# First-layer token blocks of 512 and 384 in turn instead of 448, and buffers handed to the second layer by name

## The chip, the cores and the metric

One core of one Trainium2 chip. The metric is device time in microseconds (us) of one execution. TensorE (PE in the profile) does the matrix products, VectorE (DVE) and ScalarE (ACT) the elementwise work, GpSimd (POOL) almost nothing, and SyncE (SP) issues all DMA transfers.

## The reference

Attention over 4 batches, 8 heads, 576 positions and 64 features per head, with two kinds of masks (a local window of 32, and every 32nd position), and then two feed-forward layers over all 4 x 576 = 2304 tokens with 512 features and 2048 hidden units:

```python
attn_out = _attn_ref(**attn_kwargs)                     # masked softmax attention
x = attn_out.transpose(0, 2, 1, 3).reshape(B * S, H * D)   # 2304 x 512
h = x @ w_in                                            # first layer, 512 -> 2048
g = h * np.tanh(softplus(h))
x = (g @ w_out).astype(np.float32)                      # 2048 -> 512
h = x @ w2_in                                           # second layer
g = h - np.tanh(h)
out = (g @ w2_out).astype(np.float32)
```

The weights of both layers come as 64-bit floats and are turned into 32-bit ones on the chip.

## The kernel before

**Arithmetic.** Every 32-bit operand of a large product is split into a high part and a rest in TensorE's reduced 32-bit format, and each product is the sum of three matmuls: high by high, rest by high, high by rest. So a tile names pairs: `xh`/`xl` (input of a layer, high and rest), `gh`/`gl` (hidden activations, high and rest), `w` (both parts in one tile).

**First layer.** The 2304 tokens are cut into blocks: two of 256 tokens, then four of 448 (`blocks[0]`, L262). The hidden dimension is cut into 16 chunks of 128 (`NC`). A *step* is one block and one chunk (`step`, L841). Its first product (`gemm1`, L849, the matmuls of L855) adds up 4 parts of the input features with 3 matmuls each, into a PSUM bank `h`; the block's tokens are the columns that are streamed, the weights are stationary. ScalarE makes the activation `B` (L874), `gh` is a copy of it (L451 on VectorE or L449 on ScalarE), `gl` a subtraction (L455 on VectorE). The second product (`gemm2`, L900, the matmuls of L906) streams `gh` and `gl` against 4 weight tiles, again 3 matmuls each, into four PSUM banks `acc0` to `acc3` that add up over the 16 chunks. So a step has 12 + 12 matmuls of as many columns as its block has tokens. On TensorE the first product of a step alternates with the second product of the step two before (`LAG`). After a block's last chunk the four banks are moved out (`ev`, L922) and stored.

**Attention** is laid between the steps of the first blocks; it ends in the middle of the second block of 448.

**Second layer.** Blocks of 512 tokens, four of them, and one of 256 (`blocks[1]`). A *unit* (`unit`, L1227) is one block and 256 hidden units. Its first product (L1244) is done in seven products of a two-by-two scheme with 6 matmuls of 256 columns each, into banks `hx`; sums of these on VectorE give `H`; then `th` = tanh (L1332, ScalarE), `H - th` (L1337, VectorE), and `gh`, `gl` as above. Its second product (L1381) has `gh`/`gl` as stationary operand and streams 512 columns of weights, 12 matmuls for each half `i` of the unit, into the same four banks `acc0` to `acc3`.

**Places.** Tiles share places by tags. A step `s` writes `B{s%2}`, `gh{s%2}`, `gl{s%2}`. A unit writes, for its half `i`, `H` into `B{i}`, `th` and later `gl` into `gl{i}`, `gh` into `gh{i}`. So the first unit's half 0 takes the places that the step before the last left, and half 1 those of the very last step, whose second product reads `gh1` and `gl1` to its end. The input of a block sits in `xh{J%2}`, `xl{J%2}` (L800, L801), and `tiles` (L1146) puts the second layer's input into these and some other places.

**Order.** The program is written by a planner (`Plan`, L55). Each piece of work is a task with a cost on each engine that could do it, a key (when it is due), the tasks that it comes after and the places that it takes. `run` (L131) repeatedly takes the task that can start first by these costs and writes it to its engine. Each engine then does its instructions strictly in the order written; real dependences (also those on places) are kept by semaphores whatever the planner thought. `pe_cost` (L218) is its cost of a matmul, `due` (L356 to L366) the due times. A unit takes what its predecessor left from the tables `g_free` (the task after which the places `gh` and `gl` are free) and `t_done` (the one after which `B` is free): `old = g_free.get((prev, i))` and `low1, low2`. Only units enter themselves there, so for the very first unit, whose predecessor is a step of the first layer, both are empty, and the planner takes its places to be free.

Of the kernel before, what the change touches and what calls it, by code (L numbers as in the profile page):

```python
# [9 lines left out]
F32R = mybir.dt.float32r  # L10
# [46 lines left out]
class Plan:  # L57
# [15 lines left out]
    def add(self, engs, fn, key, after=(), take=(), give=(), dma=None, start=0.0, rows=128, table=None, bulk=False):  # L73
        t = Task(engs, fn, key, take, give, dma, start)
        t.bulk = bulk
        t.table = table
        t.seq, t.rows = len(self.tasks), rows
        for a in after:
            if a is not None:
                t.wait += 1  # L80
                a.next.append(t)
        self.tasks.append(t)
        return t
# [132 lines left out]


def pe_cost(n):  # L218
    return 0.0004375 * n + 0.007


def act_cost(n, psum=False, extra=0):
# [11 lines left out]
def copies(n, psum=False):  # L234
    return {ACT: act_cost(n, psum), DVE: dve_cost(n, not psum)}


def pairs_of(n):
    return {DVE: dve_cost(n)}
# [3 lines left out]
def attention_two_moe(  # L243
# [14 lines left out]
    KC = DM // 128  # L258
    NC = 16
    WIN = 32  # L260
    scale = 1.0 / float(D) ** 0.5
    blocks = [[256, 256, 448, 448, 448, 448], [512] * 4 + [256]]  # L262
    TB = 448
    LAG = 2

    const = ctx.enter_context(tc.tile_pool(name="const", bufs=1))
# [18 lines left out]
    def sb(shape, dt, slot, name):  # L285
        return one.tile(shape, dt, tag=slot, name=name)
# [66 lines left out]
    NU, HALF = NC // 2, 256  # L353
# [4 lines left out]
    for l, j, c in steps:  # L358
        if l == 0 and j == 0:
            t_ = max(t_, FIRST + PACE * c)  # L360
        due.append(t_)
        if l == 0:
            t_ += 24 * pe_cost(blocks[l][j]) + (ATTEND if 1 < j < 5 else 0.0)
        else:
            t_ += (42 if blocks[1][j] > HALF else 24) * pe_cost(HALF) + 6 * blocks[1][j] // 128 * pe_cost(DM)
# [81 lines left out]
    def copy(e, out, in_):  # L447
        if e == ACT:
            nc.scalar.activation(out=out, in_=in_, func=ACTF.Copy)  # L449
        else:  # L450
            nc.vector.tensor_copy(out=out, in_=in_)  # L451

    def two(e, out, a, b, op):
        eng = nc.gpsimd if e == POOL else nc.vector
        eng.tensor_tensor(out=out, in0=a, in1=b, op=op)  # L455

    def sub(e, out, a, b):
        two(e, out, a, b, ALU.subtract)
# [330 lines left out]
    xh, xl = {}, {}  # L789
# [3 lines left out]
    def x_split(l, j, p, after, src, buf, key):  # L793
        n = blocks[l][j]
        J = len(blocks[0]) * l + j
        old = [] if J < 2 else [last_g1[J - 2]]

        def high(e):
            if J not in xh:
                xh[J] = sb([128, KC, TB], F32R, f"xh{J % 2}", "xh")  # L800
                xl[J] = sb([128, KC, TB], F32R, f"xl{J % 2}", "xl")  # L801
            copy(e, xh[J][:, p, :n], src())

        def low(e):
            sub(e, xl[J][:, p, :n], src(), xh[J][:, p, :n].bitcast(F32))

        a = add(copies(n), high, key, list(after) + old, give=[buf])
        b = add(pairs_of(n), low, key, [a], give=[buf])
        split.setdefault(J, {})[p] = (a, b)
# [29 lines left out]
    g1_end, B_done, g2_end = {}, {}, {}  # L839
# [271 lines left out]
    xq = {}  # L1111
    x_ready = {}

    def unit_of(place, k):

        if len(place) == 1:
            return place[0][1][:, k:k + 1]
        return place[k][1]

    def factors(j, key, ready):  # L1120
        J = len(blocks[0]) + j
        t0 = starts[1][j]
        old = [last_g1[J - 2]] + list(ready)
        raw = {}

        def load_of(x):

            lower, half = x
            a0 = t0 + HALF * half
            cut = []  # L1130
            for i, (a, m) in enumerate(pieces2):
                lo, hi = max(a, a0), min(a + m, a0 + HALF)
                if lo < hi:
                    cut.append((i, lo, hi, a))
            buf = Buf(TMP, 2 if x == X22 else 1)

            def load(e):
                raw[x] = t = sb([128, 2, HALF], F32, buf.slot, "xraw")
                for k in range(2):
                    for i, lo, hi, a in cut:  # L1140
                        nc.sync.dma_start(out=t[:, k, lo - a0:hi - a0], in_=x2d[2 * lower + k, i][:, lo - a:hi - a])

            after = [x2_store[2 * lower + k, 0, i[0] + 1] for k in range(2) for i in cut] + old
            return add({SP: 0.9 * len(cut)}, load, key - 5 + len(raw_loads), after, take=[buf], dma=0.7), buf

        def tiles():  # L1146

            if J in xq:
                return xq[J]
            one_ = lambda t: [(slice(0, 2), t)]  # L1150
            two_ = lambda a, b: [(slice(0, 1), a), (slice(1, 2), b)]
            cols = lambda t: t.rearrange("p (k n) -> p k n", n=HALF)
            a, b = (sb([128, 7, HALF], F32R, f"x{x}{J % 2}", "xq") for x in "hl")
            hi = [one_(t[:, 2 * i:2 * i + 2]) for t in (a, b) for i in range(3)] + [two_(a[:, 6:], b[:, 6:])]
            if J % 2 == 0:
                slots = ("q0", "q1", "k0", "k1", "xr0")
                lo = [one_(sb([128, 2, HALF], F32R, slot, "xq")) for slot in slots]
                t = sb([128, 4, HALF], F32R, "v", "xq")
                lo += [one_(t[:, :2]), one_(t[:, 2:])]
            else:  # L1160
                t = sb([128, 9, HALF], F32R, "pp", "xq")
                lo = [one_(t[:, 2 * i:2 * i + 2]) for i in range(4)]
                lo += [one_(cols(W2[u, 3][:, 1, :])) for u in (2 * NS, 2 * NS + 1)]
                lo += [two_(*(sb([128, 1, HALF], F32R, f"pT{i}", "xq") for i in range(2)))]
            xq[J] = list(zip(hi, lo))
            return xq[J]

        X11, X12, X21, X22 = (0, 0), (0, 1), (1, 0), (1, 1)
        raw_loads = {}
        plain = blocks[1][j] == HALF  # L1170
        for x in (X11, X21) if plain else (X11, X12, X22, X21):
            raw_loads[x] = load_of(x)
        ld = {x: r[0] for x, r in raw_loads.items()}
        bufs = {x: r[1] for x, r in raw_loads.items()}
        pc, cc = pairs_of(2 * HALF), copies(2 * HALF)
        out_ = {}

        def parts_of(i, x, after, key, last):


            def high(e):
                for k, t in tiles()[i][0]:
                    copy(e, t, raw[x][:, k])

            def low(e):
                hi, lo = tiles()[i]
                if len(hi) == len(lo):
                    for (k, h), (_, t) in zip(hi, lo):
                        sub(e, t, raw[x][:, k], h.bitcast(F32))
                else:  # L1190
                    for k in range(2):
                        sub(e, unit_of(lo, k), raw[x][:, k:k + 1], unit_of(hi, k).bitcast(F32))

            h = add(cc, high, key, after)
            out_[i] = add(pc, low, key + .1, [h], give=[bufs[x]] if last else ())
            return out_[i]

        def combine(o, a, b, after, key, give=()):
            return add(pc, lambda e: two(DVE, raw[o], raw[a], raw[b], ALU.subtract), key, after, give=give)

        x_ready[J] = out_
        if plain:
            for i, x in enumerate((X11, X21)):
                parts_of(i, x, [ld[x]] + old, key + .5 * i, True)
            return


        x11 = parts_of(0, X11, [ld[X11]] + old, key, False)
        t1 = combine(X11, X12, X11, [x11, ld[X12]], key + .2)
        t3 = combine(X12, X22, X12, [t1, ld[X22]], key + .3)  # L1210
        x22 = parts_of(2, X22, [ld[X22]] + old, key + .4, False)
        t2 = combine(X22, X22, X11, [t3, x22], key + .5)
        parts_of(4, X22, [t2], key + .6, True)
        parts_of(5, X12, [t3], key + .7, True)
        parts_of(3, X11, [t2], key + .8, True)
        x21 = parts_of(1, X21, [ld[X21]] + old, key + .9, False)
        t4 = combine(X21, X21, X22, [x21, t2], key + 1, [bufs[X22]])
        parts_of(6, X21, [t4], key + 1.1, True)
# [6 lines left out]
    t_done, g_free = {}, {}  # L1225
# [188 lines left out]
    with tc.manual_schedule():  # L1414
# [23 lines left out]
        for J in range(2, last + 1):  # L1438
# [5 lines left out]
            if J == last:  # L1444

                d5, ends = due[NC * J], [x_store[p, B - 1] for p in range(KC)]
                x = y = None
# [7 lines left out]
        for u in range(NU):  # L1455
# [4 lines left out]
            home(u, 2, [g2_end[at]], k_, d + 8)  # L1460
            home(u, 3, [g2_end[at + 1]], k_, d + 12)
        s2 = NC * (last + 1)
        done_i = [x for k in kept_i.values() for x in k]
        done_o = [x for k in kept_o.values() for x in k]
        more = [done_i + done_o + ends, done_i + done_o + [w2_in[u, 3] for u in (2 * NS, 2 * NS + 1)]]
# [9 lines left out]
        x, y = LATE  # L1475
# [58 lines left out]
```

## Time and profile before

| | us |
|---|---|
| median of 3 runs (904.09 to 904.32) | 904.22 |
| the profiled execution's own time | 905.22 |
| its span, first to last instruction | 903.4 |
| TensorE busy in the span | 892.1 (99%) |
| VectorE busy | 585.3 (65%) |
| ScalarE busy | 424.1 (47%) |

The mean granted clock of TensorE is 0.996 of full speed. Matmuls are pipelined: a matmul's listed duration is the time from its start to the modelled end of its own data, longer than the distance to the next one's start. What one costs in a row of matmuls is therefore read from starts, or from the chain of work, which lists how long a run of matmuls kept the engine.

### The profile page before, as it was taken

Reading aid. Unit: us, or ns where it says so; the run is one execution under the profiler, and the core shown is the slowest. Engines: PE = TensorE matmul, PEld = TensorE weight load, DVE = VectorE, ACT = ScalarE, POOL = GpSimd, SP = SyncE. Lnnn points to the kernel's source line nnn. Section 1 sums busy time; section 2 is a strip of 40 time slices with the busy share of each in tenths; the row PEclk is TensorE's granted clock in tenths of the full one; section 3 lists DMA queues with packets and bytes.
Section 4 is the critical chain, followed back from the end, with each engine's and each line's share of the span. In section 5 each row is a group of like instructions: output and inputs, shape, how many; then the busy total and the mean of one; then the engine's idle time right before and its main releaser. Section 6 shows DMA issues by size and latency. Waiting matters only on the chain.

```text
span 903.4 us, 16481 instructions
## 1 busy us (share of the span) xinstructions
PE 892.1 (99%) x6080; PEld 800.5 (89%) x6080; DVE 585.3 (65%) x1562; ACT 424.1 (47%) x928; POOL 2.4 (0%) x13
## 2 busy tenths in 40 slices
PE   8999999999999999999999899999999999999998
PEld 7899999888888899999999889998989999899897
DVE  6999978655455658777777466575458455545543
ACT  6999987645455525444544242242224222322211
POOL 1000000000000000000000000000000000000000
PEclk9999999999999999999999989999999999999999
DMA  9981122512131059888975253352335233644532
GB/s 292 376 344 37 48 92 88 165 53 64 53 114 43 5 208 297 272 256 272 295 225 171 77 164 105 106 178 102 103 113 181 94 111 123 198 153 167 174 127 71
DMA packets 85233, 138.19 MB, mean 153 GB/s; under 512 B 11104, under 2 KB 38752, under 8 KB 85152
## 3 DMA queue, kind: packets, MB, share of 16 engines
q1 hardware_dynamic: 85152, 137.14, 45.7%
q8 instruction: 48, 0.79, 0.3%
q14 instruction: 33, 0.27, 0.1%
HBM read 107.22 MB, written 29.88 MB: 152 GB/s over the span
## 4 chain that ended last, share of the span: by engine, by line
PE 91%; ACT 3%; DMA 3%; DVE 1%; SPq 1%; issue 0%; ACTq 0%
PE acc L1381 22%; PE acc L906 21%; PE h L855 21%; PE hx L1244 18%; PE hx L1261 3%; PE ops L715 2%; PE sps L589 2%; PE ptps L697 1%; DMA kT<-in_k_dram 1%; ACT L193 1%; DMA stwo<-in_moe_w_out_dram 1%; ACT p L645 1%; DMA stwi<-in_moe_w_in_dram 1%; DMA qT<-in_q_dram 0%; DMA vs<-in_v_dram 0%
## 5 line engine op out<-in xcount | busy, mean ns | idle before, releaser
L855 PE MATMUL h<-xh,wi 128*128 128x448 f32 (+1 forms) x768 | 219.3, 346 | 0.9 <-ACT B L874 0.9
L906 PE MATMUL acc<-gh,wo 128*128 128x448 f32 (+1 forms) x768 | 198.4, 344 | 0.0
L1381 PE MATMUL acc<-w,gh 128*128 128x512 f32 x576 | 181.2, 396 | 2.9 <-ACT ev L922 2.9
L1244 PE MATMUL hx<-xq,w 128*128 128x256 f32 x1280 | 174.3, 285 | 0.0
L1244 PEld LDWEIGHTS hx<-xq,w 128*128 128x128 f32 x1280 | 168.1, 191 | 6.7
L855 PEld LDWEIGHTS h<-xh,wi 128*128 128x128 f32 x768 | 139.2, 189 | 12.6 <-ACT B L874 1.5
L906 PEld LDWEIGHTS acc<-gh,wo 128*128 128x128 f32 x768 | 134.1, 189 | 10.4
L855 PE MATMUL h<-xl,wi 128*128 128x448 f32 (+1 forms) x384 | 130.3, 339 | 0.1
L906 PE MATMUL acc<-gl,wo 128*128 128x448 f32 (+1 forms) x384 | 130.1, 339 | 0.0
L1381 PEld LDWEIGHTS acc<-w,gh 128*128 128x128 f32 x576 | 104.2, 190 | 22.1 <-ACT ev L922 3.8
L1381 PE MATMUL acc<-w,gl 128*128 128x512 f32 x288 | 113.1, 393 | 0.0
L1332 ACT ACTIVATE th<-hx 128x256 f32<-128x256 f32 x48 | 18.5, 385 | 163.6 <-PE hx L1244 123.8
L874 ACT ACTIVATE B<-h 128x448 f32<-128x448 f32 (+1 forms) x96 | 46.8, 491 | 95.5 <-PE h L855 90.7
L1337 DVE SCALAR_TENSOR_TENSOR H<-hx,th 128x256 f32<-128x256 f32 x48 | 20.3, 424 | 104.3 <-ACT th L1332 104.2
L455 DVE TENSOR_TENSOR gl<-B,gh 128x448 fp32r<-128x448 f32 (+1 forms) x96 | 53.2, 555 | 50.0 <-ACT gh L449 47.9
L1332 ACT ACTIVATE th<-H 128x256 f32<-128x256 f32 (+1 forms) x64 | 33.4, 524 | 98.1 <-PE acc L1381 50.7
L455 DVE TENSOR_TENSOR H<-H,hx 128x256 f32<-128x256 f32 x160 | 66.9, 418 | 16.5 <-PE hx L1244 9.0
L855 PEld LDWEIGHTS h<-xl,wi 128*128 128x128 f32 x384 | 72.6, 189 | 4.3 <-DVE xl L455 0.3
L906 PEld LDWEIGHTS acc<-gl,wo 128*128 128x128 f32 x384 | 72.4, 189 | 4.5
L193 ACT ACT_TABLE_LOAD x58 | 74.4, 1283 | 1.0
L1381 PEld LDWEIGHTS acc<-w,gl 128*128 128x128 f32 x288 | 54.6, 190 | 12.4 <-DVE gl L455 0.2
L1337 DVE SCALAR_TENSOR_TENSOR H<-H,th 128x256 f32<-128x256 f32 (+1 forms) x64 | 35.6, 558 | 44.0 <-ACT th L1332 44.0
(117 smaller groups left out, 1026.7 us busy)
## 6 DMA issues: line engine op xcount, KB each, us to landing
w<-w2o SPq DMA_DIRECT2D x160, 256.0 KB, 2.8
stwi<-in_moe_w_in_dram SPq DMA_DIRECT2D x16, 512.0 KB, 8.4
stwo<-in_moe_w_out_dram SPq DMA_DIRECT2D x16, 512.0 KB, 9.0
w2v<-in_moe_w_out_dram SPq DMA_DIRECT2D x32, 256.0 KB, 3.7
w2o<-p SPq DMA_DIRECT2D x48, 128.0 KB, 3.2
w<-w2i SPq DMA_DIRECT2D x24, 256.0 KB, 2.8
out_dram<-ev SPq DMA_DIRECT2D x18, 256.0 KB, 3.9
w2v<-in_moe_w_in_dram SPq DMA_DIRECT2D x8, 512.0 KB, 4.4
```

The costliest lines, as they stand in the source:

```text
L193: self.load_table(t.table)
L455: eng.tensor_tensor(out=out, in0=a, in1=b, op=op)
L589: nc.tensor.matmul(s[a][:, at_, :], tq[64 * a:64 * a + 64, q0:q0 + nq], tk[64 * a:64 * a + 64, k0_:k0_ + nk], start=not lean, stop=not lea ...
L715: nc.tensor.matmul(o[64 * hh:64 * hh + 64, u - u0, :], vv, h["pT", a][:, at_, :], start=True, stop=True,)
L855: nc.tensor.matmul(h_ps[s], w[:, wp, kc, :], xx[:, kc, :n], start=(kc == first_kc and i == 0), stop=(kc == last_kc and i == 2),)
L874: nc.scalar.activation(out=b_tile(), in_=h_ps[s], func=ACTF.Mish, scale=2.0 ** -8)
L906: nc.tensor.matmul(acc[f][:, cols], w[:, wp, 128 * f:128 * f + 128], g, start=(opens and i == 0), stop=(closes and i == 2),)
L1244: nc.tensor.matmul(st[t], w[:, wp, 256 * i + 128 * k:256 * i + 128 * k + 128], unit_of(xq[J][x][xp], k)[:, 0], start=(q in (1, 6, 7, 5) an ...
L1261: nc.tensor.matmul(st[t], w[:, wp], unit_of(xq[J][kc // 2][xp], kc % 2)[:, 0], start=(kc == 0 and m == 0), stop=(kc == KC - 1 and m == 2),)
L1332: nc.scalar.activation(out=st["th", i][:, cols], in_=x, func=ACTF.Tanh, scale=2.0 ** -8)
L1337: nc.vector.scalar_tensor_tensor(out=st["H", i][:, cols], in0=x, scalar=2.0 ** -8, in1=st["th", i][:, cols], op0=ALU.mult, op1=ALU.subtract,)
L1381: nc.tensor.matmul(acc[f], g[:, 128 * f:128 * f + 128], where[wp](), start=(opens and m == 0), stop=(closes and m == 2),)
```

## The change

Four edits. The late blocks of the first layer are 512, 384, 512, 384 tokens instead of 448 each, so blocks of even number have 512 and those of odd number 384; the input tiles `xh0`, `xl0` become larger and `xh1`, `xl1` smaller. `tiles` places the second layer's input accordingly (even blocks no longer use the place `xr0`, odd ones do, and no longer use the places of the attention's `pT`). The planner's cost of a matmul is a table for 256, 384 and 512 columns. And the last two steps of the first layer are entered in `g_free` and `t_done`, as if they were the two halves of a unit.

```diff
--- before.py
+++ after.py
@@ -216,7 +216,7 @@
 
 
 def pe_cost(n):
-    return 0.0004375 * n + 0.007
+    return {256: 0.12, 384: 0.174, 512: 0.227}.get(n, 0.0004375 * n + 0.007)
 
 
 def act_cost(n, psum=False, extra=0):
@@ -259,8 +259,8 @@
     NC = 16
     WIN = 32
     scale = 1.0 / float(D) ** 0.5
-    blocks = [[256, 256, 448, 448, 448, 448], [512] * 4 + [256]]
-    TB = 448
+    blocks = [[256, 256, 512, 384, 512, 384], [512] * 4 + [256]]
+    TB = (512, 384)
     LAG = 2
 
     const = ctx.enter_context(tc.tile_pool(name="const", bufs=1))
@@ -797,8 +797,8 @@
 
         def high(e):
             if J not in xh:
-                xh[J] = sb([128, KC, TB], F32R, f"xh{J % 2}", "xh")
-                xl[J] = sb([128, KC, TB], F32R, f"xl{J % 2}", "xl")
+                xh[J] = sb([128, KC, TB[J % 2]], F32R, f"xh{J % 2}", "xh")
+                xl[J] = sb([128, KC, TB[J % 2]], F32R, f"xl{J % 2}", "xl")
             copy(e, xh[J][:, p, :n], src())
 
         def low(e):
@@ -1150,14 +1150,15 @@
             one_ = lambda t: [(slice(0, 2), t)]
             two_ = lambda a, b: [(slice(0, 1), a), (slice(1, 2), b)]
             cols = lambda t: t.rearrange("p (k n) -> p k n", n=HALF)
-            a, b = (sb([128, 7, HALF], F32R, f"x{x}{J % 2}", "xq") for x in "hl")
-            hi = [one_(t[:, 2 * i:2 * i + 2]) for t in (a, b) for i in range(3)] + [two_(a[:, 6:], b[:, 6:])]
+            m = TB[J % 2] // 128
+            a, b = (sb([128, 2 * m, HALF], F32R, f"x{x}{J % 2}", "xq") for x in "hl")
+            hi = [one_(t[:, 2 * i:2 * i + 2]) for t in (a, b) for i in range(m)]
             if J % 2 == 0:
-                slots = ("q0", "q1", "k0", "k1", "xr0")
-                lo = [one_(sb([128, 2, HALF], F32R, slot, "xq")) for slot in slots]
+                lo = [hi.pop()] + [one_(sb([128, 2, HALF], F32R, slot, "xq")) for slot in ("q0", "q1", "k0", "k1")]
                 t = sb([128, 4, HALF], F32R, "v", "xq")
                 lo += [one_(t[:, :2]), one_(t[:, 2:])]
             else:
+                hi += [one_(sb([128, 2, HALF], F32R, "xr0", "xq"))]
                 t = sb([128, 9, HALF], F32R, "pp", "xq")
                 lo = [one_(t[:, 2 * i:2 * i + 2]) for i in range(4)]
                 lo += [one_(cols(W2[u, 3][:, 1, :])) for u in (2 * NS, 2 * NS + 1)]
@@ -1460,6 +1461,8 @@
             home(u, 2, [g2_end[at]], k_, d + 8)
             home(u, 3, [g2_end[at + 1]], k_, d + 12)
         s2 = NC * (last + 1)
+        for i in range(2):
+            g_free[s2 - 1, i], t_done[s2 - 1, i] = g2_end[s2 - 2 + i], B_done[s2 - 2 + i]
         done_i = [x for k in kept_i.values() for x in k]
         done_o = [x for k in kept_o.values() for x in k]
         more = [done_i + done_o + ends, done_i + done_o + [w2_in[u, 3] for u in (2 * NS, 2 * NS + 1)]]
```

The number of matmuls stays: 16 chunks x 24 for each of the four late blocks, 1536 before and after, half of them now of 512 columns and half of 384.

Where the new order differs most is the hand-over between the layers. On ScalarE before, from the first tanh of the second layer (L1332) to the last move out of the first layer's banks (L922); `hx_6317` and `H_6337` belong to half 0 of the first unit, `H_6356` to its half 1, `hx_6399` and later names to the second unit:

```order
L1332 ACTIVATE th_6389<-hx_6317 128x256
L1332 ACTIVATE th_6407<-H_6356 128x512
L1332 ACTIVATE th_6389<-H_6337 128x256
L449 ACTIVATE gh_6436<-H_6337 128x512
L922 ACTIVATE ev_6448<-acc_5643 128x448
L449 ACTIVATE H_6454<-hx_6399 128x256
L922 ACTIVATE ev_6457<-acc_5655 128x448
L922 ACTIVATE ev_6463<-acc_5661 128x448
L922 ACTIVATE ev_6471<-acc_5672 128x448
```

The same stretch of the changed kernel, where `th_6389` is half 0 and `th_6463` half 1 of the first unit (line numbers are one higher behind L1153):

```order
L1333 ACTIVATE th_6389<-hx_6289 128x256
L1333 ACTIVATE th_6389<-H_6317 128x256
L449 ACTIVATE w2_6345<-w2_6345 128x256
L449 ACTIVATE H_6439<-hx_6398 128x256
L922 ACTIVATE ev_6444<-acc_5662 128x384
L922 ACTIVATE ev_6451<-acc_5669 128x384
L1333 ACTIVATE th_6463<-H_6360 128x512
L922 ACTIVATE ev_6471<-acc_5675 128x384
L922 ACTIVATE ev_6474<-acc_5681 128x384
```

Half 1's tanh stood second, ahead of half 0's second piece and of all four moves out (`ev`); now half 0's two pieces come first, and two of the four moves out stand ahead of half 1's tanh.

On VectorE before, from the first `H - th` to the last `gl` of the first unit (`H_6337` is half 0, `H_6356` half 1):

```order
L1337 SCALAR_TENSOR_TENSOR H_6337<-hx_6317,th_6389 128x256
L1337 SCALAR_TENSOR_TENSOR H_6356<-H_6356,th_6407 128x512
L1337 SCALAR_TENSOR_TENSOR H_6337<-H_6337,th_6389 128x256
L451 CAST gh_6434<-H_6356 128x512
L455 TENSOR_TENSOR gl_6438<-H_6356,gh_6434 128x512
L455 TENSOR_TENSOR gl_6443<-H_6337,gh_6436 128x512
```

And with the change (`H_6317` is half 0, `H_6360` half 1; `w2` tiles are second-layer weights brought in for later units):

```order
L1338 SCALAR_TENSOR_TENSOR H_6317<-hx_6289,th_6389 128x256
L1338 SCALAR_TENSOR_TENSOR H_6317<-H_6317,th_6389 128x256
L455 TENSOR_TENSOR w2_6345<-w2_6345 128x256
L451 CAST gh_6425<-H_6317 128x512
L455 TENSOR_TENSOR gl_6434<-H_6317,gh_6425 128x512
L455 TENSOR_TENSOR H_6439<-H_6439,hx_6407 128x256
L451 CAST w2_6380<-w2_6380 128x512
L455 TENSOR_TENSOR w2_6380<-w2_6380 128x512
L1338 SCALAR_TENSOR_TENSOR H_6360<-H_6360,th_6463 128x512
L451 CAST gh_6481<-H_6360 128x512
L455 TENSOR_TENSOR gl_6488<-H_6360,gh_6481 128x512
```

Half 0 went through behind half 1; now half 0 is finished, with its `gh` and `gl`, before half 1's subtraction.

## Rows read from the trace of the kernel before

**Rows 1.** The page's busy times: TensorE.

```profile
PE 892.1 (99%) x6080; PEld 800.5 (89%) x6080; DVE 585.3 (65%) x1562; ACT 424.1 (47%) x928; POOL 2.4 (0%) x13
```

**Rows 2.** The page's chain that ended last, shares of the span by engine.

```profile
PE 91%; ACT 3%; DMA 3%; DVE 1%; SPq 1%; issue 0%; ACTq 0%
```

**Rows 3.** The chain in order of time (start us, us, what), four runs of matmuls.

```profile
83.97 1.44 PE acc L906 x12
...
342.91 2.48 PE acc L906 x12
...
565.71 2.75 PE acc L1381 x12
...
863.03 2.87 PE hx L1261 x24
```

**Rows 4.** TensorE's timeline (start us, us, instructions), 559.80 to 562.55 us.

```profile
559.80 0.63 PE L1381 MATMUL acc<-w,gh 128*128 128x512 f32 x2
...
561.19 0.62 PE L1381 MATMUL acc<-w,gh 128*128 128x512 f32 x2
...
562.55 3.16 PE L1244 MATMUL hx<-xq,w 128*128 128x256 f32 x24
```

**Rows 5.** TensorE's timeline between attention work, nine matmuls from 184.30 to 186.12 us.

```profile
184.30 0.56 PE L906 MATMUL acc<-gh,wo 128*128 128x448 f32 x2
...
186.12 0.41 PE L697 MATMUL ptps<-ident,p 96*128 96x96 f32 x3
```

**Rows 6.** Stretches: us, PE, PEld, DVE, ACT, POOL busy (instructions), PE clock, DMA.

```profile
166.00:326.00 160.00, 160.00 (x1065) 139.03 (x1064) 86.50 (x349) 81.62 (x126) 0.00 (x0) 1.00 0.23 75
326.00:503.95 177.95, 177.95 (x862) 161.60 (x861) 134.64 (x311) 82.70 (x174) 0.00 (x0) 1.00 0.77 249
422.00:503.95 81.95, 81.95 (x398) 74.42 (x397) 59.84 (x134) 38.64 (x81) 0.00 (x0) 1.00 0.73 234
```

**Rows 7.** The chain in order of time at the hand-over between the layers.

```profile
514.63 2.45 PE acc L906 x12
...
517.11 0.64 ACT th L1332
...
517.77 1.04 DVE H L1337 x2
...
518.83 0.63 ACT gh L449
519.46 0.44 ACT ev L922
...
519.94 5.70 PE acc L1381 x12
525.65 2.51 PE hx L1244 x18
```

**Rows 8.** ScalarE's timeline at the hand-over, idle time before a row in brackets.

```profile
510.30 0.38 ACT L1332 ACTIVATE th<-hx 128x256 f32<-128x256 f32 x1 [2.27 <-PE hx L1244]
517.11 0.94 ACT L1332 ACTIVATE th<-H 128x512 f32<-128x512 f32 x2 [6.42 <-PE acc L906]
518.83 0.63 ACT L449 ACTIVATE gh<-H 128x512 fp32r<-128x512 f32 x1 [0.79 <-DVE H L1337]
519.37 0.53 ACT L922 ACTIVATE ev<-acc 128x448 f32<-128x448 f32 x1
520.57 0.38 ACT L449 ACTIVATE H<-hx 128x256 f32<-128x256 f32 x1 [0.67 <-DVE gl L455]
520.85 1.41 ACT L922 ACTIVATE ev<-acc 128x448 f32<-128x448 f32 x3
```

**Rows 9.** Two stretches at the hand-over, columns as in rows 6.

```profile
517.07:519.94 2.87, 0.00 (x0) 0.00 (x0) 2.07 (x5) 2.00 (x4) 0.00 (x0) 0.93 0.00 0
519.94:525.65 5.71, 5.71 (x13) 4.14 (x14) 2.70 (x6) 1.69 (x4) 0.00 (x0) 0.50 0.54 184
```

**Rows 10.** Who TensorE waited for: us in total, times, longest us; three of seven.

```profile
PE acc L1381 <- ACT ev L922: 2.9, 1, 2.9
...
PE ops L715 <- DMA vs<-in_v_dram: 0.9, 1, 0.9
PE h L855 <- ACT B L874: 0.9, 2, 0.6
```

## The prediction, made before the changed kernel ran

> **What bounds the kernel now.** I read the busy times first: TensorE is busy 892.1 of 903.4 us, the next engine, VectorE, 65% [rows 1]. Busy alone proves little for pipelined matmuls, so the chain that ended last comes next: 91% of it is TensorE [rows 2]. Then the waits of TensorE: it stopped in few places, longest once for 2.9 us at the hand-over between the layers, then 0.9 us each for a load and an activation [rows 10]. So there are two ways to a shorter time: matmuls that follow each other at a shorter distance, and that one stop. The change touches both.
>
> The distance from start to start is read from runs of matmuls in the chain. Twelve of 448 columns keep the engine 2.48 us, 206.7 ns each; twelve of 256 take 1.44 us, 120.0 ns each, and in the second layer 24 take 2.87 us, 119.6 ns; twelve of 512 take 2.75 us, 229.2 ns [rows 3]. The timeline splits the last: the first six of the run take 1.39 us (561.19 - 559.80), the last six 1.36 us, 226.7 ns each [rows 4]. From 256 to 512 columns that is 106.7 ns more for 256 columns, one cycle of 2.4 GHz each; the columns alone then make 106.7, 186.7 and 213.3 ns for 256, 448 and 512. What is paid on top is 13.3 ns at 256, 13.3 ns at 512 and 20.0 ns at 448. The size of 448 stands off the line through the other two by 6.7 ns.
>
> **Part 1: 512 and 384 instead of 448.** No row shows 384 columns with these operands. The line through 256 and 512 gives 173.3 ns; the other bound is the extra of 448, 180.0 ns. I take 173.3: 384, 512 and 256 are all multiples of 128 and 448 is not, the only property I see that sets 448 apart; the same line of code has 120.0 ns with 256 columns, so it is not the line's role [rows 3]. A pair of 448s (413.3 ns) becomes 226.7 + 173.3 = 400.0 ns, 13.3 less; 1536 matmuls are 768 pairs: 10.2 us. With 180.0 ns it would be 5.1 us.
>
> Two deductions come from the stretch with attention, where matmul runs are cut by other work. From 326 us on 862 matmuls take 177.95 us, 206.4 ns each, all at the long distance [rows 6]; in 12s these are 71 runs or 852, which leaves 684 of 1536 to the attention stretch. There, after an interruption, 448s run shorter: nine in 1.82 us, 202.2 ns [rows 5]. If half of the 684 do (an estimate from such runs), 342 x 4.5 ns = 1.5 us are already earned today. And the first six 512s behind other work cost 0.03 us more than the last six [rows 4]; the new order has some 33 interruptions in the first block of 512, so 1.0 us. Both ends: 7.7 and 10.2 us; I take 8.2, nearer to the lower end because both effects stand in rows.
>
> The work of the other engines per token is the same, in pieces of other sizes; it lies beside TensorE, which never stops from 326 to 504 us while VectorE is busy 134.64 of 177.95 us [rows 6]. If that cover went, the first thing late would be the second layer's weights and input (last rival). The second layer's blocks read whole pieces of 512 now, so a few loads fall away on SP; nothing waits for them.
>
> **Part 2: the hand-over.** Here a chain stands in place of TensorE: the last second product of the first layer ends, then a tanh of 0.64 us, two subtractions 1.04, `gh` 0.63, `ev` 0.44, and 2.88 us after its end TensorE starts again [rows 7]. ScalarE had been idle 6.42 us before that tanh, waiting for the last product [rows 8]: it is half 1's, whose place `gl1` that product still reads, and it stands ahead of half 0's second piece and of all `ev`s, as the planner believed the place free. Behind the stop, the granted clock is 0.50, the 1.2 GHz level [rows 9]: twelve 512s take 5.70 instead of 2.75 us, the next 18 of 256 take 2.51 instead of 18 x 0.1196 = 2.15 us [rows 3, 7]. Sum: 2.88 + 2.95 + 0.36 = 6.2 us.
>
> In the new order half 0's tanh, subtraction, `gh` and `gl` no longer stand behind half 1. What is late next? Count from the start of the last second product of the first layer: 12 x 173.3 ns, its end is at 2.08 us, its four banks are done at 0.52, 1.04, 1.56, 2.08. Two `ev`s (0.53 us at most; three in a row take 1.41 [rows 8]) end near 1.2 and 1.75. Then comes half 1's tanh, which must wait for 2.08 and ends at 2.75 with the 0.64 of [rows 7]; the other two `ev`s end near 3.2 and 3.65. TensorE wants the banks at 2.08, 2.76, 3.44 and 4.12 (three 512s each, 0.68 us). So the wait that the change adds, that tanh ahead of two `ev`s, has 0.2 to 0.5 us to spare. Cost: at least 0, at most 0.6 us (`ev`s one tanh later than thought); I take 0.2. So short a stop should not have the lower clock behind it: in the stop of 2.88 us the mean grant is still 0.93, so it fell only in the last 0.4 us of it [rows 9]. Gain 6.0 us, ends 5.6 and 6.2.
>
> **Part 3: new costs in the planner.** They shift the order of some work from the first blocks on. The number of times that attention work breaks into large products is 94 before and after. I take 0, with 1.5 us either way, the size of the other stops [rows 10].
>
> **Sum.** The profiled execution took 905.2 us, 903.4 of span and 1.8 around it. 905.2 - 8.2 - 6.0 = 891.0. The median of the runs is 1.0 lower than the profiled one: **890.0**.
>
> **Rivals.**
> - *384 is no better than 448 on top of its columns* (180.0 ns): 5.1 us less, 895.1. For it: no row of that size; against it: 256 and 512. 12 in 100.
> - *Every matmul pays one fixed amount whatever its size*, so that equal numbers of matmuls and equal columns give equal time: only the hand-over pays, 905.2 - 6.0 - 1.0 = 898.2. Against it: 20.0 ns beside 13.3 in rows [rows 3, 4]. 4 in 100. The Trainium skill states such a rule (page "TensorE: Matmul & The Clock Gate", section "Back-to-back issue gap": columns over 2.4 GHz plus about 2.5 ns once warm); by it 448 takes 189.2 ns and a pair of 512 and 384 the same as two of 448, and part 1 would be worth nothing. Here the trace differs with 206.7 ns.
> - *The stop stays*: half 1's tanh, the weights that ScalarE and VectorE now convert between the pieces, or a late load hold the `ev`s or `gl`, TensorE stops for 1.5 us or more and part of the lower clock comes back. Half of part 2 lost: 893.0, all of it: 896.0. Against it the counts above, each with little to spare. 9 in 100.
> - *Slower: the last block is too short for what must be ready behind it.* A block of 384 lasts 16 x 24 x 173.3 ns = 66.6 us, not 79.4. In the last 81.95 us before the second layer VectorE works 59.84 us [rows 6], much of it on second-layer weights and input. If the same work lay in 66.6 us it would be 90% busy, and TensorE would wait from the point where 66.6 is passed, 6.8 us more work. To come out slower by over 0.2%, TensorE would have to wait 14.2 + 1.8 = 16.0 us: some 23 us of work moved there from the block before, which itself gets 7.6 us longer. Then 906 or more. 3 in 100.
>
> **How the numbers follow.** The forecast has 70 in 100, with a range of its own of 886.5 to 892.5 (part 1 from 7.7 to 10.2, part 2 from 5.6 to 6.2, part 3). The remaining 2 in 100 are for no difference, by something not thought of. The range takes in the best ends (905.2 - 10.2 - 6.2 - 1.5 - 1.0 = 886.3) and the first and third rival: 886.0 to 895.8. About 0.2% or 1.8 us is what measuring this kernel can tell from no change. Faster than that are the forecast and the first three rivals: 95 in 100; within it 2; slower 3.
>
> **What would show it.** Runs of twelve in the chain at L906 and L855 of 2.72 us (512) and 2.08 us (384) say that part 1 is right; 2.16 us for 384 is the first rival, 2.80 and 2.16 the second. No stop of TensorE ahead of the first second product of the second layer, and a granted clock of 1.00 there, say that part 2 is right; `ev` or `gl` as releaser with over 1 us is the third rival. TensorE stopping behind VectorE from 400 to 495 us would be the last. The prediction is wrong in its base if the time between 25 and 166 us, where only 256 columns run, changes by more than 2 us.

## The result, and the profile after

The changed kernel takes 892.17 us, median of 4 runs (891.31 to 892.59), the kernel before 904.15 us (903.41 to 904.32): ratio 0.9868, 95% interval 0.9851 to 0.9885. That is 12.0 us less. Forecast were 890.0 us and 14.2 us less; the time lies 2.2 us above the forecast, within its range.

The page of the changed kernel, busy times:

```profile
PE 882.3 (99%) x6080; PEld 788.3 (89%) x6080; DVE 593.0 (67%) x1578; ACT 429.3 (48%) x910; POOL 2.4 (0%) x13
```

Against [rows 1], TensorE still is the bound, at the same share, with 9.8 us less of listed work in as many matmuls. The chain in order of time shows the new distances (start us, us, what), and then the hand-over:

```profile
379.95 2.72 PE h L855 x12
...
480.27 2.08 PE h L855 x12
...
501.86 5.08 PE hx L1245 x42
506.94 2.08 PE acc L906 x12
509.02 2.78 PE acc L1382 x12
511.80 0.71 PE hx L1245 x6
```

Twelve of 512 columns take 2.72 us, 226.7 ns each, twelve of 384 take 2.08 us, 173.3 ns each: both on the line through 256 and 512 that [rows 3, 4] gave. At the hand-over the chain of [rows 7] through ScalarE and VectorE is gone. The first second product of the second layer (L1382 here) follows the last of the first layer at once, in 2.78 us instead of 5.70.

ScalarE's timeline at the hand-over (idle before a row in brackets):

```profile
502.61 0.38 ACT L1333 ACTIVATE th<-hx 128x256 f32<-128x256 f32 x1 [3.69 <-PE hx L1245]
504.50 0.42 ACT L1333 ACTIVATE th<-H 128x256 f32<-128x256 f32 x1 [1.51 <-DVE H L455]
504.82 0.40 ACT L449 ACTIVATE w<-w 128x256 fp32r<-128x256 f32 x1
506.87 0.38 ACT L449 ACTIVATE H<-hx 128x256 f32<-128x256 f32 x1 [1.64 <-DVE gl L455]
507.50 1.01 ACT L922 ACTIVATE ev<-acc 128x384 f32<-128x384 f32 x2 [0.25 <-PE acc L906]
509.06 0.63 ACT L1333 ACTIVATE th<-H 128x512 f32<-128x512 f32 x1 [0.55 <-PE acc L906]
509.60 0.85 ACT L922 ACTIVATE ev<-acc 128x384 f32<-128x384 f32 x2
```

Where [rows 8] had ScalarE idle for 6.42 us ahead of half 1's tanh with everything else behind it, both pieces of half 0 and two `ev`s now come first, and the wait ahead of half 1's tanh is 0.55 us. The last two `ev`s end at 510.45, and TensorE never waits for them.

Stretches (us, PE, PEld, DVE, ACT, POOL busy (instructions), PE clock, DMA):

```profile
501.86:509.02 7.16, 7.16 (x55) 7.16 (x55) 4.56 (x11) 2.48 (x6) 0.00 (x0) 1.00 0.13 45
509.02:511.80 2.78, 2.78 (x15) 2.20 (x14) 1.83 (x4) 1.39 (x3) 0.00 (x0) 1.00 0.81 282
...
326.00:494.83 168.83, 168.83 (x856) 153.65 (x856) 130.49 (x305) 78.11 (x167) 0.00 (x0) 1.00 0.79 257
```

The granted clock stays at 1.00 through the hand-over, against 0.93 and 0.50 in [rows 9]. From 326 us to the first matmul of the second layer VectorE is busy 77% of the time, 76% before [rows 6]: the work of the second layer's weights fits beside the shorter last block. TensorE's waits no longer name `ev`. Of those left, these two lie between 16 and 59 us from the start, and this execution lists none behind them:

```profile
PE ptps L697 <- ACT dd L735: 0.8, 2, 0.5
...
PE h L855 <- ACT B L874: 0.5, 1, 0.5
```

To say where the time went, each trace is cut by starts of matmuls: the first of the first layer (L855), the first of the late blocks (the 448s, or the 512s and 384s), the one in which the late blocks have streamed 680000 of their 688128 columns (just ahead of the hand-over), and the last of all. In us; second and third are repeats, and e1 and e2 have one part of the change each, all told of below:

| kernel, profiled execution | first at | to the first late block | to 680000 columns | to the last matmul | span |
|---|---|---|---|---|---|
| before, shown above | 30.51 | 125.85 | 351.61 | 391.55 | 903.4 |
| before, second (e8) | 29.90 | 125.89 | 351.58 | 390.09 | 901.4 |
| before, third (e9) | 30.38 | 126.43 | 351.62 | 390.11 | 902.4 |
| changed, shown above | 30.12 | 126.48 | 343.37 | 385.40 | 889.5 |
| changed, second (e3) | 31.35 | 126.61 | 343.36 | 385.52 | 891.0 |
| changed, third (e10) | 31.22 | 126.45 | 343.37 | 385.39 | 890.6 |
| sizes alone (e1) | 30.91 | 126.40 | 343.35 | 390.72 | 895.6 |
| hand-over alone (e2) | 30.26 | 125.89 | 351.46 | 385.39 | 896.9 |

The late blocks take 8.2 us less, in every pair of rows of the kernel before and the changed one. The part with the hand-over takes 6.15 us less than in the execution that the prediction read, and 4.7 us less than in the two others.

### The profile page after: what moved, and what is told of

Its sections match the earlier page's. It is cut to its first block, busy times and chain, and to the rows that moved or that the text cites. A ratio compares the mean times of both kernels' runs of the same rounds, so it can differ in the third digit from the quotient of the medians.

```text
span 889.5 us, 16480 instructions
## 1 busy us (share of the span) xinstructions
PE 882.3 (99%) x6080; PEld 788.3 (89%) x6080; DVE 593.0 (67%) x1578; ACT 429.3 (48%) x910; POOL 2.4 (0%) x13
## 4 chain that ended last, share of the span: by engine, by line
PE 93%; ACT 4%; DVE 1%; DMA 1%; issue 0%; SPq 0%; ACTq 0%
PE acc L1382 22%; PE h L855 22%; PE acc L906 22%; PE hx L1245 18%; PE hx L1262 3%; PE sps L589 2%; PE ops L715 2%; PE ptps L697 2%; ACT p L645 1%; DMA kT<-in_k_dram 1%; ACT stwo L402 0%; ACT pT L449 0%; ACT L193 0%; ACT stwi L402 0%; ACT dd L735 0%
## 5 line engine op out<-in xcount | busy, mean ns | idle before, releaser
L855 PE MATMUL h<-xh,wi 128*128 128x256 f32 (+2 forms) x768 | 215.1, 342 | 0.6 <-ACT B L874 0.5
L906 PE MATMUL acc<-gh,wo 128*128 128x256 f32 (+2 forms) x768 | 196.5, 341 | 0.0
L1382 PE MATMUL acc<-w,gh 128*128 128x512 f32 x576 | 179.1, 392 | 0.0
L855 PEld LDWEIGHTS h<-xh,wi 128*128 128x128 f32 x768 | 137.9, 189 | 14.4 <-ACT B L874 1.0
L906 PEld LDWEIGHTS acc<-gh,wo 128*128 128x128 f32 x768 | 132.1, 189 | 10.4
L855 PE MATMUL h<-xl,wi 128*128 128x256 f32 (+2 forms) x384 | 129.4, 337 | 0.1
L906 PE MATMUL acc<-gl,wo 128*128 128x256 f32 (+2 forms) x384 | 128.9, 336 | 0.0
L1382 PEld LDWEIGHTS acc<-w,gh 128*128 128x128 f32 x576 | 103.2, 188 | 18.1 <-DVE gh L451 0.4
L1382 PE MATMUL acc<-w,gl 128*128 128x512 f32 x288 | 112.2, 389 | 0.0
L874 ACT ACTIVATE B<-h 128x256 f32<-128x256 f32 (+2 forms) x96 | 46.9, 492 | 89.5 <-PE h L855 87.0
L455 DVE TENSOR_TENSOR gl<-B,gh 128x256 fp32r<-128x256 f32 (+2 forms) x96 | 52.9, 553 | 46.6 <-ACT gh L449 44.1
L1333 ACT ACTIVATE th<-H 128x256 f32<-128x256 f32 x64 | 33.5, 524 | 95.2 <-PE acc L1382 51.0
L855 PEld LDWEIGHTS h<-xl,wi 128*128 128x128 f32 x384 | 72.5, 189 | 5.0 <-DVE xl L455 0.3
L1382 PEld LDWEIGHTS acc<-w,gl 128*128 128x128 f32 x288 | 54.1, 188 | 12.1 <-DVE gl L455 0.2
L1338 DVE SCALAR_TENSOR_TENSOR H<-H,th 128x256 f32<-128x256 f32 x64 | 35.7, 558 | 40.2 <-ACT th L1333 39.9
```

The lines of the kernel that those rows point to most:

```text
L855: nc.tensor.matmul(h_ps[s], w[:, wp, kc, :], xx[:, kc, :n], start=(kc == first_kc and i == 0), stop=(kc == last_kc and i == 2),)
L874: nc.scalar.activation(out=b_tile(), in_=h_ps[s], func=ACTF.Mish, scale=2.0 ** -8)
L906: nc.tensor.matmul(acc[f][:, cols], w[:, wp, 128 * f:128 * f + 128], g, start=(opens and i == 0), stop=(closes and i == 2),)
L1333: nc.scalar.activation(out=st["th", i][:, cols], in_=x, func=ACTF.Tanh, scale=2.0 ** -8)
L1338: nc.vector.scalar_tensor_tensor(out=st["H", i][:, cols], in0=x, scalar=2.0 ** -8, in1=st["th", i][:, cols], op0=ALU.mult, op1=ALU.subtract,)
L1382: nc.tensor.matmul(acc[f], g[:, 128 * f:128 * f + 128], where[wp](), start=(opens and m == 0), stop=(closes and m == 2),)
```

## The experiments

**Each part alone.** Is the stop a matter of the block sizes, and do the parts add? First the sizes without the hand-over (e1):

```diff
-        for i in range(2):
-            g_free[s2 - 1, i], t_done[s2 - 1, i] = g2_end[s2 - 2 + i], B_done[s2 - 2 + i]
```

> Blocks of 512 and 384, without the entry of the last steps in the hand-over tables. If the two parts add (sizes 8.2 us, hand-over 6.0 us): 8.2 us under the kernel before, some 896 us, and the stop of TensorE of about 2.9 us with the half clock behind it is still there. If the parts do not add, because the stop comes from the block size: below 892.5 us and no stop. If the sizes are worth less in the runs than in the profiled execution: 898 us or more.

Measured: 897.23 us, ratio 0.9909 (0.9881 to 0.9937), 7.0 us under the 904.26 us of the kernel before on this chip. The stop is there. TensorE's timeline has it ahead of a row, and the stretches show the clock during and behind it:

```profile
512.73 0.74 PE L1382 MATMUL acc<-w,gh 128*128 128x512 f32 x2 [3.00 <-ACT ev L922]
```

```profile
509.70:512.73 3.03, 0.03 (x2) 0.00 (x1) 2.28 (x5) 2.77 (x6) 0.00 (x0) 1.00 0.00 0
512.73:517.40 4.67, 4.41 (x13) 3.16 (x14) 2.49 (x6) 1.53 (x4) 0.00 (x0) 0.71 0.56 195
517.40:522.75 5.35, 5.35 (x33) 4.86 (x32) 2.62 (x6) 1.74 (x4) 0.00 (x0) 0.94 0.46 151
```

Here the whole stop still has the full clock; the lower level (1.2 GHz) comes only after TensorE has started again. So the price of a stop does not end with it.

Then the hand-over with blocks of 448 (e2), the same two lines added to the kernel before:

```diff
+        for i in range(2):
+            g_free[s2 - 1, i], t_done[s2 - 1, i] = g2_end[s2 - 2 + i], B_done[s2 - 2 + i]
```

> Blocks of 448 as before, with the entry in the hand-over tables. If the parts add: 6.0 us under the kernel before, some 898 us; matmuls of 448 columns still 206.7 ns apart, no stop over 0.3 us at the hand-over, granted clock 1.00 there. If the half clock was not a consequence of the stop: only 2.9 us, some 901 us, and the clock still falls.

Measured: 899.26 us, ratio 0.9946 (0.9918 to 0.9974), 5.0 us under the kernel before. Its chain and its stretches:

```profile
514.27 2.43 PE acc L906 x12
516.70 2.72 PE acc L1381 x12
```

```profile
509.19:516.70 7.51, 7.51 (x55) 7.33 (x55) 4.74 (x10) 2.28 (x5) 0.00 (x0) 1.00 0.18 54
516.70:519.42 2.72, 2.72 (x15) 2.25 (x14) 1.86 (x4) 1.06 (x2) 0.00 (x0) 1.00 0.86 307
```

No stop, no lower clock: two lines in the planner's tables take away both, so the stop was the planner's not knowing, and the clock followed the stop. The parts add: 7.0 + 5.0 = 12.0 us, and the changed kernel in the same comparison has 12.1. Both medians are about 1 us under what the prediction had, but their intervals (5.7 to 10.8 and 2.4 to 7.4 us) are too wide to tell that; the stretches are not. In e1 the late blocks take 343.35 us, 8.2 less; the part with the hand-over takes 390.72, 0.6 more than in the second and third execution of the kernel before (e8, e9), and what lies behind the last matmul 0.3 more. In e2 the part with the hand-over takes 385.39 us, 4.7 less than in e8 and e9, and the late blocks 351.46.

**Is it the execution that was read?** The changed kernel once more, unaltered (e3):

> The changed kernel unaltered. If its profiled execution of 891.31 us was a fast one by chance: another profiled execution of 891.5 to 893 us, the difference sitting before the first late block or in waits for transfers, and a ratio near 0.987. If it repeats within 0.3 us, the gap of 1.9 us between the change of the profiled executions (13.9) and of the medians (12.0) comes from the profiled execution of the kernel before.

Measured: 892.16 us, ratio 0.9869 (0.9831 to 0.9908). The profiled execution took 892.81 us, 1.5 more than the first one, and by the table above 1.4 of it lies ahead of the late blocks (31.35 and 30.12 us for the first matmul). The kernel before, a second time (e8) and a third (e9), and the changed one a third (e10):

> The kernel before, unaltered, for a second profiled execution. If the profiled execution shown before was long by the clock behind the stop: the same stop of 2.9 us, and fewer matmuls at the half clock behind it. If it was long by its first loads: the first matmul of the first layer earlier than 30.5 us.

> The kernel before, unaltered, a third profiled execution. If executions of this kernel differ by the start (first matmul of the first layer, 29.9 and 30.5 us so far) and by how long the half clock lasts behind the stop (the twelve matmuls there took 4.64 and 5.70 us so far), and by nothing else: the stretch from the first late block to 680000 columns is 351.6 us again, and span less those two parts is the same within 0.2 us.

> The changed kernel, a third profiled execution. By the same theory it differs from the first two only at the start: 343.4 us from the first late block to 680000 columns, 385.4 to 385.5 us from there to the last matmul, no stop and no half clock.

Measured: 903.14, 904.22 and 892.48 us. The changed kernel's third execution came out as expected, without a stop behind the first late matmul. In e8 both causes that I had named show: its first matmul comes 0.6 us earlier, and its part with the hand-over is 1.45 us shorter. The chain of the second execution at the hand-over, and its stretches:

```profile
518.88 0.44 ACT ev L922
...
519.37 4.64 PE acc L1381 x12
524.00 2.15 PE hx L1244 x18
526.15 2.75 PE acc L1381 x12
```

```profile
516.49:519.37 2.88, 0.00 (x1) 0.01 (x1) 2.08 (x5) 2.00 (x4) 0.00 (x0) 0.97 0.00 0
519.37:524.00 4.63, 4.63 (x14) 3.36 (x15) 2.70 (x6) 1.69 (x4) 0.00 (x0) 0.65 0.61 209
524.00:528.90 4.90, 4.90 (x33) 4.41 (x32) 2.61 (x6) 1.74 (x4) 0.00 (x0) 1.00 0.57 180
```

And the chain of the third:

```profile
520.40 4.72 PE acc L1381 x12
525.12 2.15 PE hx L1244 x18
```

The stop is the same 2.9 us, but the clock is back before the twelve matmuls are through: 4.64 and 4.72 us where [rows 7] had 5.70, and the 18 behind them at full speed. The stop cost 2.88 + 1.89 = 4.8 us here and 6.2 us in the execution that I read. My expectation that all else is constant held within 0.04 us for the late blocks, and failed by 0.6 us for the stretch ahead of them (126.43 against 125.85).

**The planner's new costs.** The changed kernel with the old cost formula (e5):

```diff
-    return {256: 0.12, 384: 0.174, 512: 0.227}.get(n, 0.0004375 * n + 0.007)
+    return 0.0004375 * n + 0.007
```

> The changed kernel with the planner's old formula for a matmul's cost. If the new cost of 256 columns (0.120 in place of 0.119) is what made the stretch from the first matmul of the first layer to the first late block longer (125.9 us before, 126.4 to 126.6 with the change): 125.9 us again there, and 0.5 us faster than the changed kernel, some 891.6 us, unless the old costs of 512 and 384 give a worse order later. If that stretch is longer by chance: no difference to the changed kernel there.

The kernel before with the new table in place of the formula, the same edit the other way (e6):

> The kernel before with the new cost table alone (448 by the old formula). If the new cost of 256 columns lengthens the early stretch: 126.5 us there and 0.6 us slower than the kernel before. If not: 125.9 us and the same time. The late blocks and the hand-over as in the kernel before either way, with the stop and the half clock.

And the changed kernel with the old cost for 256 columns alone (e7):

```diff
-    return {256: 0.12, 384: 0.174, 512: 0.227}.get(n, 0.0004375 * n + 0.007)
+    return {384: 0.174, 512: 0.227}.get(n, 0.0004375 * n + 0.007)
```

> The changed kernel with the old cost for 256 columns and the new ones for 384 and 512. If both of the last theories hold (the cost of 256 lengthens the early stretch, those of 384 and 512 keep the later order as it is): 125.9 us in the early stretch and 0.5 us faster than the changed kernel, some 891.6 us. Otherwise 892.2 us or more.

| kernel | us (ratio, interval) | to the first late block | to 680000 columns |
|---|---|---|---|
| changed, old costs (e5) | 892.92 (0.9859, 0.9827 to 0.9890) | 126.19 | 344.47 |
| changed, old cost of 256 (e7) | 892.38 (0.9855, 0.9827 to 0.9884) | 125.91 | 344.34 |
| before, new costs (e6) | 903.26 (0.9982, 0.9957 to 1.0007) | 127.29 | 349.01 |

The medians of e5 and e7 cannot be told from the changed kernel's, so neither gave the 0.5 us that I expected. The stretches say why: with the old cost of 256 the early stretch is 0.3 to 0.6 us shorter than in the changed kernel, and the one behind it, with attention in its first half, 1.0 to 1.1 us longer. In the kernel before, the new costs alone (e6) give 2.6 us in that stretch and lose 1.4 us in the early one, against my expectation that the late blocks would stay as they were.

Between e7 and the changed kernel only one cost differs, 0.119 and 0.120 us: that moves attention work across the boundary of the two stretches. Of the 1200 attention matmuls (L586 to L731) 480 lie behind the first late one in the kernel before, in e5 and in e7, 464 in the changed kernel, and 448 in e6. So a good part of what one stretch gains the other loses: both together take 469.8 to 470.0 us in the changed kernel, 470.2 in e7, 470.7 in e5, and 476.3 in e6 against 477.5 to 478.1 in the kernel before. The new costs are then worth 0.2 to 0.9 us with the new blocks and 1.2 to 1.7 us with the old ones; the medians do not tell either from nothing. The third execution of the kernel before has 126.43 us in the early stretch without the moved work, so executions differ there by as much as that work takes.

**Other sizes.** What sets 448 apart (e4)?

```diff
-    blocks = [[256, 256, 512, 384, 512, 384], [512] * 4 + [256]]
-    TB = (512, 384)
+    blocks = [[256, 256, 480, 416, 464, 432], [512] * 4 + [256]]
+    TB = (512, 432)
...
-    TMP = [f"tmp{x}" for x in range(5)]
+    TMP = [f"tmp{x}" for x in range(4)]
...
-        rb, tb = Buf(["xr0", "tmp4"], 1), Buf(["p3", "p4"], 1)
+        rb, tb = Buf(["xr0", "tmp3"], 1), Buf(["p3", "p4"], 1)
```

> Late blocks of 480, 416, 464 and 432 tokens and one temporary place less. If the extra of 6.7 ns of 448 columns falls on every size that is no multiple of 128: distances of 220.0, 193.3, 213.3 and 200.0 ns (columns over 2.4 GHz plus 20.0). If it falls on sizes that are no multiple of 64 or 32 in different amounts, 480 and 416 differ from 464 and 432. If 448 alone is odd: 213.3, 186.7, 206.7 and 193.3 ns (plus 13.3).

Measured: 899.02 us in one run, which also has 3.5 us more ahead of the late blocks than the changed kernel (129.95 us) and is no price of the distances alone. The chain, one run of twelve for each size in the order 480, 416, 464, 432:

```profile
224.11 2.60 PE h L855 x12
...
335.68 2.26 PE h L855 x12
...
388.86 2.51 PE h L855 x12
...
462.09 2.34 PE h L855 x12
```

These are 216.7, 188.3, 209.2 and 195.0 ns, on top of the columns at 2.4 GHz 16.7, 15.0, 15.8 and 15.0 ns. None of the three outcomes that I had written down: these four sizes lie between the 13.3 ns of 256, 384 and 512 and the 20.0 of 448. Multiples of 128 are the cheapest of the eight, and 448 is the dearest, which "no multiple of 128" does not explain. Why 448 is so is open. The four new figures are means: at 416 and 432 single distances go up and down between 183 and 199 ns.

## Why the prediction was right, and where it was off

**The distances** held in each number: 226.7 ns for 512 and 173.3 ns for 384, so neither the rival of 180.0 ns nor that of one fixed amount for every size came to pass. The Trainium skill's formula behind that last rival (page "TensorE: Matmul & The Clock Gate", section "Back-to-back issue gap", which gives it for a matmul in isolation) would, as an estimate, have 189.2 ns for 448 and nothing to gain from the sizes; this trace has 206.7.

**Part 1** was put at 8.2 us and the late blocks took 8.2 us less. Part of this agreement is luck. Worked out from the starts between the first late block and the last attention work, with the settled distance of each size (206.7, 226.7, 173.3) taken off: 448s that stood inside runs were 1.6 us short in all before, and 512s and 384s are 0.8 + 0.2 us long now. That is 2.7 us to be deducted from 10.2, the full 1.5 + 1.0 of my lower end and a little more, where I took 2.0. Another 0.6 us goes where a matmul of one size follows one of another, which I had not counted. Of the 10.1 us that the settled distances give up to 680000 columns some 6.8 are left, under my lower end of 7.7. The other 1.5 us came from the order, which I had put at 0 with 1.5 us either way. About half of it is the stop for a load in [rows 10], which lies among the late blocks of the kernel before:

```profile
164.17 0.74 PE L715 MATMUL ops<-pT,vs 72*64 72x72 f32 x16 [0.91 <-DMA vs<-in_v_dram]
```

It is there in all three executions of that kernel, and with 0.7 us in e2; the changed kernel, e1, e5, e6 and e7 have none there. The other half is mostly the 16 attention matmuls that now stand ahead of the first late block, where they take time too. With all 480 behind its start, in e5 and e7, the late blocks gain 7.1 to 7.3 us.

**Part 2** was right in what happens, from ScalarE's order to the clock, and the count of the new wait was close: TensorE reached the third bank about 0.2 us after its `ev` was done, by ScalarE's row (0.85 us for two from 509.60, so the first is done near 510.05) and its own start:

```profile
510.25 0.62 PE L1382 MATMUL acc<-w,gh 128*128 128x512 f32 x2
```

The size of part 2 was off. "Gain 6.0 us" came from one execution; 6.15 us is what that execution gives, 4.7 us what the two others give, and e2 has 5.0 in the medians. The part that varies is how long the lower clock lasts behind one and the same stop. The execution that I read was the unusual one: its mean granted clock is 0.996, while e8, e9 and every other recorded run of that kernel between 903.0 and 905.5 us with a clock beside it have 0.998. My reason why a short stop keeps the full clock was not put to the test: no stop was left, and in e1 the clock fell only behind the stop.

**The sum** then used that same microsecond twice. I took the profiled execution's 905.2 us, subtracted the whole price of its long half clock, and subtracted 1.0 more "for the median". But the long half clock is a large part of why this execution lay above the median (1.45 us more than in e8 and e9), and the change removes it; what is left has no such offset. Without that step the sum is 891.0, 0.3 us from the profiled execution of the changed kernel, 891.31. The median of 892.17 lies 0.9 us above that one, which had an early start among its kind: 30.12 us for the first matmul, against 31.35 and 31.22.

**Part 3**, other order elsewhere, was 0 with 1.5 us either way. The time from the start to the first late block is 156.36, 155.79, 156.81 and 156.15 us in four executions of the old early order (before, e8, e9, e2), and 156.59, 157.96, 157.67 and 157.31 us in four of the new (changed, e3, e10, e1): 1.1 us later on average, with ranges that overlap. Some 0.6 us of it is the first matmul's start, where TensorE's order is the same in all; it lies between 29.90 and 31.35 us, and why it differs was not found. The other 0.5 us is where the 16 moved attention matmuls are. The sign that I had set for a wrong base, over 2 us there, did not come.

By means over the profiled executions, then: 8.2 us from the late blocks, 5.1 from the part with the hand-over (390.6 and 385.4), 1.1 given back ahead of them and 0.3 behind the last matmul (span less the four columns), 11.9 us, against 12.0 measured. With the 4.7 us of the usual clock in place of 5.1 it is 11.5, so the last half microsecond is not pinned down.

**The other rivals.** A stop that stays did not come. The last block too short for VectorE did not come either: 77% busy, and no wait of TensorE between 326 us and the hand-over.

**Three readings to set right.** TensorE's waits before also had two of 1.0 us in the first 10 us, which I passed over; the change does not touch them. The 448s begin at 156.4 us, so 256 columns run alone until then and not until 166. And in the changed kernel the odd blocks' input still uses the places of `pT`; what `xr0` replaces is the pair of last parts of `xh1` and `xl1`.

## What to carry to other kernels

Read the distance of matmuls from runs of them, per size, before choosing block sizes: equal columns in as many matmuls were worth about 7 us here, because one size paid 20.0 ns on top of its columns and two others 13.3. Where a planner writes the order, look where two stages share places: an engine that takes work in order and is given first what must wait holds everything behind it, and the stop that follows cost 4.8 to 6.2 us here for a length of 2.88, through the clock. Where work can move from one stretch to another, count it on both sides before calling a shorter stretch a gain. And where one profiled execution lies above the median, ask which of its terms makes it so before carrying that difference over to the changed kernel.

## What the runs showed of the hardware that was not expected

- On top of columns at 2.4 GHz, a matmul in a settled run of this reduced 32-bit kind costs 13.3 ns at 256, 384 and 512 columns, 15.0 at 416 and 432, 15.8 at 464, 16.7 at 480 and 20.0 at 448. At 448 the settled distance of 206.7 ns is longer than the 202 ns behind interruptions [rows 5]; at 512 it is the other way (231.7 and 226.7 ns in [rows 4]).
- The same stop of 2.9 to 3.0 us is followed by different lengths at the lower clock: twelve 512s took 5.70, 4.64 and 4.72 us in three executions of one kernel. In e1 the clock was full for the whole stop and fell after it.
- A change of 0.001 us in one planner cost (256 columns, e7 against the changed kernel) took 1.0 us off the late blocks and put 0.6 us on the stretch ahead of them, with as many matmuls in all: 16 of attention's changed sides.
